# Second batch of an attention and mixture-of-experts kernel: the sign of a head's hash placed directly behind the hash

## The chip, the cores and the metric

The kernel runs on one core of a Trainium2 chip. The metric is the device time of one execution in microseconds (us); lower is better.

## The reference, cut to what matters

Two batches (B = 2) of 8 heads, 768 rows, 64 columns go through an attention in which a row sees only the keys of its own hash bucket. The bucket is the pattern of six signs of the row times a 64x6 matrix. The result, as 1536 rows of 512, goes through a dense mixture of four experts.

```python
q_bits = (np.einsum('bhsd,dk->bhsk', q, proj) > 0)
k_bits = (np.einsum('bhsd,dk->bhsk', k, proj) > 0)
mask = q_bucket[:, :, :, None] == k_bucket[:, :, None, :]
scores = np.where(mask, scale * q @ k^T, -1e9)
attn = softmax(scores);  x = attn @ v
for e in range(4):
    out += p[:, e:e+1] * (np.maximum(x @ w1[e], 0) @ w2[e])
```

## The kernel before, in words

**Heads and steps.** The 16 heads are numbered 0 to 15 here: head 8b + h is head h of batch b. `attention()` (L557) walks through all heads in steps of one 128-row tile of scores, six steps (t = 0 to 5) to a head. In each step it gives out the parts in the order `ORDER = "TXSUVMEYNRP"`: X turns an earlier tile of exponentials on VectorE (L458), S makes the scores of this step's tile (matmuls L368 and L370 on PE, minimum L375 on VectorE), E takes the exponential of the tile one step back (L391 on ScalarE), M multiplies by the reciprocal sums on GpSimd (L533), and P, last in the step, gives out one piece of the preparation of the **next** head. All engines execute their instructions in the order in which they were given out (`tc.manual_schedule()`), so the place in this order is the place in the engine's queue.

**Preparation of a head.** `prep_head` (L283) is a generator; one piece is taken in each step's P. For heads 2 to 8 and 11 to 15 (`BLOCKS`) the pieces are: t = 0 a transpose on VectorE (L293); t = 1 the split of q and k into a high and a low part (L230 on ScalarE, L231 on VectorE) and copies on GpSimd (L221); t = 2 the hash, six matmuls on PE (L315) into a PSUM tile `hps`, and a copy on GpSimd; t = 3 the sign of the hash (L324 on ScalarE: it reads `hps` and writes the bit rows of `k2`), then two GpSimd operations that make the bit rows of the other operand (L327, L335, the latter through the helper at L221). Heads 9 and 10 are turned on PE instead (L299), and have everything one step earlier: split at t = 0, hash at t = 1, sign and GpSimd operations at t = 2. The preparation issues no DMA; the loads are given out by P itself (L619, L621). The values that the generator yields (654, 978, 0) are only a budget for the mixing described next. `mixed(b, h)` (L357) is true for heads 0 to 8.

**What runs beside it.** While batch 0's attention runs, nothing of the experts but the split of the first weights does. After that the experts of batch 0 (`moe`, L740) and the attention of batch 1 are woven together (L998 to L1008): after each block of the experts (`yield 1960`: twelve matmuls L757 to L759 into a tile `mps`, Relu L763 on ScalarE, L764 on VectorE; or `yield 2600`: twelve matmuls L697 to L699, L691 on VectorE) as many pieces of the attention are taken as the budget allows. The weights are loaded (L647), split into a high part by VectorE (L665) and a low part by GpSimd (L658) meanwhile. The experts of batch 1 (`moe_fast`) come last and alone.

**PSUM.** Two pools: `ps2` with **two** buffers (`big`, L100), which score tiles `sps`, transposes `tps` and hashes `hps` share, and `ps1` with four (`one`, L103) for all else. A buffer is given back when the last instruction that reads it is done: L375 for a score tile, L324 for a hash. Which of two free buffers a new tile gets is settled when the program is built. The next head's scores need the sign's products only at t = 0 of that head.

Of the kernel before, what the change touches and what calls it, by code (L numbers as in the profile page):

```python
# [10 lines left out]
ACTF = mybir.ActivationFunctionType  # L11
# [7 lines left out]
SGN_SCALE = float(2**20)  # L19
# [30 lines left out]
def tile_lsh_attention__then__domain_moe(  # L50
# [11 lines left out]
    nc = tc.nc  # L62
    B, H, S, D = q.shape
# [12 lines left out]
    NH = S // 2  # L76
# [3 lines left out]
    MKE = MK + 2 * NB  # L80
    scale = 1.0 / float(D) ** 0.5
# [18 lines left out]
    def big(name):  # L100
        return ps2.tile([P, 2, 512], F32, tag="big", name=name)

    def one(name):  # L103
        return ps1.tile([P, 512], F32, tag="one", name=name)
# [3 lines left out]
    sgn_bias = const.tile([P, 1], F32, name="sgn_bias")  # L108
# [11 lines left out]
    def two(t):  # L120
        return t.rearrange("p (a n) -> p a n", a=2)
# [65 lines left out]
    def in_blocks(b, h):  # L187
        return b * H + h in BLOCKS
# [27 lines left out]
    def stack_tiles(b, h):  # L216
        heads[b, h] = tuple(stk.tile([P, S], F32R, tag=n, name=n) for n in ("q1", "al", "ah", "k2"))
        return heads[b, h]

    def copy_pool(dst, src):  # L220
        nc.gpsimd.tensor_scalar(out=dst, in0=src, scalar1=1.0, scalar2=1.0, op0=ALU.mult, op1=ALU.mult)  # L221
# [7 lines left out]
    def split_half(dst_hi, dst_lo, src):  # L229
        nc.scalar.activation(dst_hi, src, ACTF.Copy, scale=qk_scale)  # L230
        nc.vector.scalar_tensor_tensor(  # L231
            out=dst_lo, in0=src, scalar=qk_scale, in1=dst_hi.bitcast(F32), op0=ALU.mult, op1=ALU.subtract
        )
# [49 lines left out]
    def prep_head(b, h):  # L283
        second = (b, h) == (0, 1)
        if not second:
            tqk = loaded.pop((0, b, h))
        q1, al, ah, k2 = stack_tiles(b, h)
        if second:
            for ps, sl in zip(in_psum, halves):
                split_half(ah[:, sl], al[:, sl], ps[:, :NH])  # L290
        elif in_blocks(b, h):
            xt = ld.tile([P, S], F32, tag="tqk", name="xt")
            nc.vector.transpose(out=xt, in_=tqk.rearrange("p c r d -> p (c r d)"))  # L293
            yield 0
            split_half(two(ah), two(al), two(xt))
        else:
            ps = big("tps")
            for c in range(NT):
                nc.tensor.transpose(  # L299
                    ps[:, c // 3, (c % 3) * P : (c % 3 + 1) * P], tqk[:, c].rearrange("p a d -> p (a d)"), ident  # L300
                )
            split_half(two(ah), two(al), ps[:, :, :NH])
        for rows in (slice(0, D), slice(D, P)):
            copy_pool(q1[rows], ah[0:D].bitcast(F32))
        copy_pool(k2[0:D], ah[D:P].bitcast(F32))
        yield 654
        if second:
            yield 0
            ps = [one("hps1") for _ in range(2)]
        else:  # L310
            hps = big("hps")
            ps = [hps[:, i] for i in range(2)]
        for j, (w, a) in enumerate(((phi, ah), (plo, ah), (phi, al))):
            for i, sl in enumerate(halves):
                nc.tensor.matmul(ps[i][:MKE, :NH], w, a[:, sl], start=j == 0, stop=j == 2)  # L315
        copy_pool(ah[0:D], al[D:P].bitcast(F32))
        if second:
            for i, sl in enumerate(halves):
                nc.scalar.activation(
                    k2[D:MKE, sl], ps[i][D:MKE, :NH], ACTF.Sign, bias=sgn_bias[D:MKE], scale=SGN_SCALE  # L320
                )
        yield 978
        if not second:
            nc.scalar.activation(  # L324
                two(k2[D:MKE]), hps[D:MKE, :, :NH], ACTF.Sign, bias=sgn_bias[D:MKE], scale=SGN_SCALE
            )
        nc.gpsimd.tensor_scalar(  # L327
            out=al[D:MKE],
            in0=k2[D:MKE].bitcast(F32),
            scalar1=1.0,  # L330
            scalar2=bit_mul[D:MKE],
            op0=ALU.add,
            op1=ALU.mult,
        )
        copy_pool(k2[MQ:MQE], al[MK:MKE].bitcast(F32))  # L335
        yield 0
# [20 lines left out]
    def mixed(b, h):  # L357
        return b * H + h < LIGHT_FROM
# [198 lines left out]
    def attention():  # L557
# [3 lines left out]
        def do(op, i):  # L561
# [24 lines left out]
            elif op == "S":  # L586
                if i < n:
                    b, h, t = seq[i]
                    if t == 0:
                        x = hseq.index((b, h))  # L590
                        prep[0] = prep_head(*hseq[x + 1]) if x + 1 < len(hseq) else iter(())
                    stage_s(b, h, t)
                    return 652 + 4270 // NT
# [446 lines left out]
```

## Time and profile before

| | us |
|---|---|
| median of 3 runs | 745.59 (745.38 to 748.12) |
| the profiled execution, its own time | 746.74 |
| its span in the trace | 744.8 |
| PE busy | 721.7 (97%) |
| VectorE (DVE) busy | 472.6 (63%) |
| ScalarE (ACT) busy | 298.7 (40%) |
| GpSimd (POOL) busy | 306.9 (41%) |

How to read it: the span is the time between the first and the last instruction that the profiler recorded. Times of rows are us from its start. Engines work side by side, so busy times don't add up to the span. In a timeline a row has start, duration, engine, line, operation, output <- input, and in brackets how long the engine sat idle before it and what it waited for. PEclk is the granted TensorE clock as a share of full speed.

### The profile page before, as it was taken

How to read it: one execution, taken by the hardware profiler on the slowest of the kernel's cores; microseconds unless marked ns; L12 is line 12 of the kernel's file. 1: busy time of each engine (PE TensorE's matmuls, PEld its weight loads, DVE VectorE, ACT ScalarE, POOL GpSimd, SP SyncE). 2: the span in 40 equal slices, each digit the busy share in tenths (PEclk: the TensorE clock that was granted, in tenths of full speed). 3: DMA queues.
4: the chain of work that ended last, by engine and by line, in shares of the span. 5: the costliest groups of instructions: out<-in, count | busy, mean ns of one | idle time of the engine just before them, and what ended most of it. 6: DMA issues, size and time to landing. Idle time of an engine off the chain costs nothing.

```text
span 744.8 us, 10164 instructions
## 1 busy us (share of the span) xinstructions
PE 721.7 (97%) x3826; PEld 615.3 (83%) x3826; DVE 472.6 (63%) x781; ACT 298.7 (40%) x592; POOL 306.9 (41%) x279
## 2 busy tenths in 40 slices
PE   8988899999989999899999999999999999999998
PEld 6766566697987897879879888998989989899896
DVE  6677676546666666568563323798667686676763
ACT  6777677633232341332422010444334343343430
POOL 5349485423415441445142324754234342343420
PEclk9999999999999999999999999999999999999999
DMA  5224323504686797769767411243021130212302
GB/s 142 44 51 85 72 60 85 85 1 129 162 206 157 213 240 180 193 164 259 217 193 211 115 58 56 67 137 109 30 86 57 63 106 30 85 58 64 105 1 85
DMA packets 85504, 83.05 MB, mean 111 GB/s; under 512 B 49872, under 2 KB 52432, under 8 KB 85456
## 3 DMA queue, kind: packets, MB, share of 16 engines
q1 hardware_dynamic: 84432, 82.08, 40.8%
q8 instruction: 30, 0.49, 0.3%
q10 hardware_dynamic: 1024, 0.33, 0.2%
q14 instruction: 18, 0.15, 0.1%
HBM read 62.68 MB, written 19.71 MB: 111 GB/s over the span
## 4 chain that ended last, share of the span: by engine, by line
PE 87%; ACT 5%; DVE 4%; DMA 2%; issue 1%; POOL 0%; SPq 0%; DVEq 0%; POOLq 0%; ACTq 0%
PE mps L697 12%; PE mps L699 12%; PE mps L698 12%; PE pv L493 9%; PE mps L758 6%; PE mps L757 6%; PE mps L759 6%; PE sps L368 4%; PE sps L370 3%; PE ptps L438 2%; PE mps L912 2%; PE mps L908 2%; PE mps L911 2%; ACT p L391 2%; PE pd L908 2%; PE pa L912 2%
## 5 line engine op out<-in xcount | busy, mean ns | idle before, releaser
L697 PE MATMUL mps<-w2hi,hh 128*128 128x512 f32 (+1 forms) x388 | 150.7, 388 | 0.0
L699 PE MATMUL mps<-w2hi,hl 128*128 128x512 f32 (+1 forms) x388 | 150.5, 388 | 0.0
L698 PE MATMUL mps<-w2lo,hh 128*128 128x512 f32 (+1 forms) x388 | 150.4, 388 | 0.0
L375 DVE TENSOR_SCALAR_CACHE_REDUCE p<-sps 128x768 f32<-128x768 f32 x96 | 90.3, 941 | 32.9 <-PE sps L370 31.2
L391 ACT ACTIVATE p<-p,nb 128x768 f32<-128x768 f32 x96 | 89.5, 932 | 42.3 <-DVE p L375 41.8
L691 DVE SCALAR_TENSOR_TENSOR acc<-mps,pe,acc 128x512 f32<-128x512 f32 (+1 forms) x85 | 63.0, 741 | 63.0 <-PE mps L699 62.6
L763 ACT ACTIVATE hh<-mps 128x384 fp32r<-128x384 f32 x64 | 31.4, 490 | 178.5 <-PE mps L759 178.5
L758 PE MATMUL mps<-xs,w1hi 128*128 128x384 f32 x256 | 87.3, 341 | 0.6 <-POOL xs L538 0.6
L757 PE MATMUL mps<-xs,w1hi 128*128 128x384 f32 x256 | 87.7, 343 | 0.0
L759 PE MATMUL mps<-xs,w1lo 128*128 128x384 f32 x256 | 87.2, 341 | 0.0
L699 PEld LDWEIGHTS mps<-w2hi,hl 128*128 128x128 f32 x388 | 72.8, 188 | 15.6
L894 POOL TENSOR_TENSOR w2lo<-ws,w2hi 128x512 fp32r<-128x512 f32 x32 | 40.5, 1286 | 108.4 <-ACT w2hi L893 108.4
L698 PEld LDWEIGHTS mps<-w2lo,hh 128*128 128x128 f32 x388 | 72.9, 188 | 13.9
L697 PEld LDWEIGHTS mps<-w2hi,hh 128*128 128x128 f32 x388 | 72.8, 188 | 13.8
L764 DVE SCALAR_TENSOR_TENSOR hl<-mps,hh 128x384 fp32r<-128x384 f32 x64 | 35.5, 555 | 73.4 <-ACT hh L763 73.1
L658 POOL TENSOR_TENSOR w1lo<-ws,w1hi 128x512 fp32r<-128x512 f32 x32 | 42.5, 1328 | 79.6 <-DVE w1hi L665 36.1
L658 POOL TENSOR_TENSOR w2lo<-ws,w2hi 128x512 fp32r<-128x512 f32 x32 | 41.2, 1289 | 69.5 <-DVE w2hi L665 55.5
L493 PE MATMUL pv<-pt,tv 128*64 128x384 f32 x288 | 67.3, 492 | 0.0
L221 POOL TENSOR_SCALAR q<-ah 64x768 fp32r<-64x768 f32 (+1 forms) x33 | 32.4, 982 | 72.0 <-ACT ah L230 70.5
L368 PE MATMUL sps<-ah,q 128*128 128x384 f32 x192 | 54.5, 365 | 6.7 <-DVE p L375 3.7
L853 POOL TENSOR_TENSOR w1lo<-ws,w1hi 128x512 fp32r<-128x512 f32 x24 | 37.9, 1588 | 35.6 <-ACT w1hi L849 22.4
L493 PEld LDWEIGHTS pv<-pt,tv 128*64 128x64 f32 x288 | 24.8, 136 | 32.2 <-issue 31.8
(135 smaller groups left out, 1432.8 us busy)
## 6 DMA issues: line engine op xcount, KB each, us to landing
ws<-in_moe_w_dram SPq DMA_DIRECT2D x64, 512.0 KB, 4.0
scr<-t SPq DMA_DIRECT2D x14, 1152.0 KB, 8.7
pt<-scr SPq DMA_DIRECT2D x56, 288.0 KB, 6.1
tv<-in_v_dram SPq DMA_DIRECT2D x16, 192.0 KB, 4.5
out_dram<-acc SPq DMA_DIRECT2D x11, 256.0 KB, 2.0
rdb<-row SPq DMA_DIRECT2D x14, 192.0 KB, 5.2
tqk<-in_q_dram SPq DMA_DIRECT2D x26, 96.0 KB, 3.3
tqk<-in_k_dram SPq DMA_DIRECT2D x24, 96.0 KB, 3.4
```

What stands on the lines that cost most here:

```text
L368: nc.tensor.matmul(ps[:, i, :NH], q1[:, sl], k1[:, i * NH : (i + 1) * NH], start=True, stop=False)
L375: nc.vector.tensor_scalar(out=two(pt), in0=ps[:, :, :NH], scalar1=MASKED, scalar2=MASKED, op0=ALU.min, op1=ALU.min, accum_out=nb,)
L391: nc.scalar.activation(pt, pt, ACTF.Exp, bias=nb, scale=-1.0, accum_out=dens[b, h, r][:, o : o + 1])
L493: nc.tensor.matmul(dst, vvs[b, h][:, c], pts[b, h, g][c], start=c == 0, stop=c == NT - 1, tile_position=(0, g * D),)
L658: nc.gpsimd.tensor_tensor(out=lo[:, c - 1], in0=st[c - 1], in1=hi[:, c - 1].bitcast(F32), op=ALU.subtract)
L691: nc.vector.scalar_tensor_tensor(out=acc, in0=ps, scalar=pcol, in1=acc, op0=ALU.mult, op1=ALU.add)
L697: nc.tensor.matmul(ps, hh[:, ts], w2hi[:, f, cs], start=n == 0, stop=False)
L698: nc.tensor.matmul(ps, hh[:, ts], w2lo[:, f, cs], start=False, stop=False)
L699: nc.tensor.matmul(ps, hl[:, ts], w2hi[:, f, cs], start=False, stop=n == FC - 1)
L757: nc.tensor.matmul(ps[:, :SB], w1hi[:, kk, fs], xhi[b, kk][:, sl], start=kk == 0, stop=False)
L758: nc.tensor.matmul(ps[:, :SB], w1hi[:, kk, fs], xlo[b, kk][:, sl], start=False, stop=False)
L759: nc.tensor.matmul(ps[:, :SB], w1lo[:, kk, fs], xhi[b, kk][:, sl], start=False, stop=kk == KD - 1)
```

## The change

Heads 9 to 15: the sign stands directly behind the hash, in the same piece, so it is given out before the next step's parts instead of behind them. Heads 0 to 8 keep the order that they had. Heads 9 and 10 also get one empty piece more (`yield 0`) ahead of the two GpSimd operations, which so come one step later than before, at t = 3, as they do in heads 11 to 15, where they stay. Nothing is added to or removed from the computation.

```diff
         yield 654
+
+        def sign():
+            nc.scalar.activation(
+                two(k2[D:MKE]), hps[D:MKE, :, :NH], ACTF.Sign, bias=sgn_bias[D:MKE], scale=SGN_SCALE
+            )
+
         if second:
             yield 0
             ps = [one("hps1") for _ in range(2)]
...
+        if not mixed(b, h):
+            sign()
         yield 978
-        if not second:
-            nc.scalar.activation(
-                two(k2[D:MKE]), hps[D:MKE, :, :NH], ACTF.Sign, bias=sgn_bias[D:MKE], scale=SGN_SCALE
-            )
+        if b and h and not in_blocks(b, h):
+            yield 0
+        if mixed(b, h) and not second:
+            sign()
         nc.gpsimd.tensor_scalar(
             out=al[D:MKE],
...
```

## Rows read from the trace of the kernel before

**Rows 1.** The page: busy time, share of the span, instructions of each engine.

```profile
PE 721.7 (97%) x3826; PEld 615.3 (83%) x3826; DVE 472.6 (63%) x781; ACT 298.7 (40%) x592; POOL 306.9 (41%) x279
```

**Rows 2.** Waits of PE over the whole span: us in total, times, longest.

```profile
PE sps L368 <- DVE p L375: 3.7, 4, 2.3
PE sps L368 <- ACT k L324: 2.4, 1, 2.4
```

**Rows 3.** Stretches: length, then busy us of PE, PEld, DVE, ACT, POOL; PEclk; DMA.

```profile
180.00:210.00 30.00, 27.59 (x145) 23.99 (x144) 20.47 (x36) 9.06 (x19) 12.54 (x11) 1.00 0.72 176
240.00:270.00 30.00, 30.00 (x166) 26.42 (x165) 19.70 (x32) 10.33 (x22) 12.16 (x11) 1.00 0.83 228
300.00:330.00 30.00, 27.66 (x139) 23.84 (x139) 18.91 (x33) 9.03 (x19) 15.94 (x14) 0.94 0.65 176
```

**Rows 4.** Line L324, the sign: duration ns min/median/max, first and last start.

```profile
L324 ACT ACTIVATE k<-hps,sgn_bias x14: 895/896/900, 27.1 to 348.1; 44x768 fp32r<-44x768 f32 x14
```

**Rows 5.** Timeline of all engines while head 11 is prepared.

```profile
201.13 0.51 PE L315 MATMUL hps<-al,phi 128*108 128x384 f32 x2
...
201.39 0.93 ACT L391 ACTIVATE p<-p,nb 128x768 f32<-128x768 f32 x1
...
203.57 0.51 PE L368 MATMUL sps<-ah,q 128*128 128x384 f32 x2
203.77 0.49 ACT L763 ACTIVATE hh<-mps 128x384 fp32r<-128x384 f32 x1 [1.36 <-PE mps L759]
...
206.59 0.49 ACT L763 ACTIVATE hh<-mps 128x384 fp32r<-128x384 f32 x1 [2.32 <-PE mps L759]
206.97 0.93 ACT L391 ACTIVATE p<-p,nb 128x768 f32<-128x768 f32 x1
...
208.01 0.90 ACT L324 ACTIVATE k<-hps,sgn_bias 44x768 fp32r<-44x768 f32 x1
...
208.96 0.61 PE L368 MATMUL sps<-ah,q 128*128 128x384 f32 x2 [2.41 <-ACT k L324]
```

**Rows 6.** Stretches behind the two longest waits of PE, columns as in rows 3.

```profile
209.80:213.40 3.60, 3.60 (x14) 3.60 (x13) 0.97 (x2) 0.00 (x0) 1.01 (x2) 0.53 1.03 228
...
308.50:312.10 3.60, 3.60 (x14) 3.60 (x13) 2.17 (x4) 0.00 (x0) 2.45 (x2) 0.57 0.18 15
```

**Rows 7.** Timeline of all engines while head 14 is prepared.

```profile
302.60 0.93 ACT L391 ACTIVATE p<-p,nb 128x768 f32<-128x768 f32 x1
302.70 0.51 PE L315 MATMUL hps<-al,phi 128*108 128x384 f32 x2
...
305.43 0.43 DVE L665 CAST w2hi<-ws 128x512 fp32r<-128x512 f32 x1 [3.59 <-DMA ws<-in_moe_w_dram]
...
306.66 0.92 DVE L375 TENSOR_SCALAR_CACHE_REDUCE p<-sps 128x768 f32<-128x768 f32 x1
...
307.65 0.61 PE L368 MATMUL sps<-ah,q 128*128 128x384 f32 x2 [2.34 <-DVE p L375]
...
315.86 0.90 ACT L324 ACTIVATE k<-hps,sgn_bias 44x768 fp32r<-44x768 f32 x1
```

**Rows 8.** Timelines, heads 9 and 13: last hash matmuls and the next on ACT.

```profile
134.14 0.51 PE L315 MATMUL hps<-al,phi 128*108 128x384 f32 x2
...
135.02 0.49 ACT L444 ACTIVATE pth<-ptps 128x384 f32<-128x384 f32 x1 [1.16 <-PE ptps L438]
...
271.04 0.51 PE L315 MATMUL hps<-al,phi 128*108 128x384 f32 x2
...
271.22 0.94 ACT L391 ACTIVATE p<-p,nb 128x768 f32<-128x768 f32 x1 [2.03 <-DVE p L375]
```

**Rows 9.** Timelines of POOL and PE, preparation and first use of head 10.

```profile
171.15 0.92 POOL L327 TENSOR_SCALAR al<-k,bit_mul 44x768 fp32r<-44x768 f32 x1 [9.55 <-ACT k L324]
...
176.36 1.27 POOL L658 TENSOR_TENSOR w1lo<-ws,w1hi 128x512 fp32r<-128x512 f32 x1 [1.34 <-DVE w1hi L665]
...
186.85 0.52 PE L370 MATMUL sps<-k,al 76*128 76x384 f32 x2
```

## The prediction, made before the changed kernel ran

> **What bounds the kernel now.** I read the page first: PE is busy for 721.7 us, 97% of the span, and the next engine for 63% [rows 1]. So PE sets the end, and a change pays only what it takes out of PE's idle time or out of the time in which PE runs slowly. Next I read PE's waits. The sign is named there once, with 2.4 us before a score matmul; the minimum L375, which frees the buffers of score tiles, with 3.7 us in four waits, the longest 2.3 us [rows 2]. Third, the stretches: from 180 to 210 us and from 300 to 330 us PE is busy for 27.59 and 27.66 of 30 us, and a stretch between them is full [rows 3]. So in the part where the changed heads are prepared there are two gaps, and almost nothing else to win. The timelines show what each gap is.
>
> *Gap 1, head 11.* The last hash matmuls end at 201.64 (201.13 + 0.51). The sign could follow, but it stands behind the next step's parts: ACT does E at 201.39, a Relu at 203.77, one at 206.59, whose block of matmuls PE has only just finished, E again at 206.97, and the sign from 208.01 to 208.91. PE wants the hash's PSUM buffer for the next score tile and sits idle for 2.41 us until 208.96 [rows 5].
>
> *Gap 2, head 14.* The hash ends at 303.21, but the sign stands only at 315.86. All that time the hash holds one of the two `big` buffers, so score tiles share the other. The score at 307.65 waits 2.34 us for the minimum of the tile before it, at 306.66, which VectorE does late because it waited 3.59 us for weights to land at 305.43 [rows 7]. The trace names L375 as the releaser, yet the reason that there was no other buffer is the late sign.
>
> Behind both gaps PE runs slowly: the granted clock is 0.53 over the next 3.60 us and 0.57 over another 3.60 us, with 14 matmuls in each [rows 6], against 1.00 in the full stretch [rows 3]. That is 1.2 GHz for most of it where it had been 2.4. The loss is (1 - 0.53) x 3.60 = 1.69 us and (1 - 0.57) x 3.60 = 1.55 us.
>
> **The change part by part.** *Sign moved, heads 9 to 15.* Its length stays 0.90 us [rows 4]; no instruction is added. On ACT it now waits for the hash, and the next step's instructions queue behind it. It starts when the hash and the E before it are done.
> - Head 11: E ends at 202.32; the sign runs until about 203.3, before the Relu of 203.77 could start. PE would find the buffer free when it comes at 206.55 (208.96 - 2.41). Gap 1 goes: -2.41, and the slow clock behind it: -1.69. Sum -4.10.
> - Head 14: E ends at 303.53; the sign runs from about 303.6 to 304.5. PE comes to the score at 305.31 (307.65 - 2.34). If the score tile takes the hash's buffer, gap 2 goes: -2.34 and -1.55. Sum -3.89. The margin is 0.8 us. What is late next: the minimum at 306.66 still comes late, but the score after it would come about two blocks and a score later, so its buffer is then free.
> - Heads 9 and 13: here something on ACT is pushed back. In head 9 the hash ends at 134.65, the sign at 135.55, and the copy that started at 135.02 starts 0.53 us later; in head 13 the hash ends at 271.55, the sign at 272.45, and the E of 271.22 starts 1.23 us later [rows 8]. Bounds: nothing, if PE does not need their results at once, and 0.53 + 1.23 = 1.76 us, if all of it lands on PE. I take nothing: the old sign stood close behind these same instructions, so ACT's total up to there is unchanged, and PE did not wait for ACT there. If that cover goes, it costs the 1.76.
> - Heads 10, 12 and 15 are like head 11: the sign would end before ACT's next instruction starts, and PE shows no gap. Taken at 0.
>
> *GpSimd operations of heads 9 and 10, a step later.* In head 10 L327 stood at 171.15 after 9.55 us of waiting for the sign; PE first needs the product at 186.85. If two weight operations come ahead of it, it starts behind 177.63 (176.36 + 1.27), and with 0.92 us of its own and as much for the copy behind it it ends near 179.5, 7 us ahead of the need [rows 9]. Cost 0, at worst as far as the weight operations are now freed from waiting behind it, a small gain off the path. In heads 11 to 15 these two keep their place and get their input earlier. SP's queue is passed by nothing, since the preparation issues no DMA and the loads keep their steps. The extra piece yields 0, so the weaving with the experts stays as it is.
>
> *The clock.* The rows show a loss behind both gaps, so I take both. A sentence apart: the Trainium skill, page "TensorE: Matmul & The Clock Gate", Part 1, says that the clock drops to 1.2 GHz when PE has been idle and that the moment is not tied to the kernel, so that the slow stretch varies between runs; by it a run of before may have paid 2.41 + 2.34 = 4.75 us for the gaps alone, and the change would be worth that much to it instead of 7.99. Both gaps of this trace agree with the drop; that it varies no row here shows.
>
> **The sum.** -4.10 - 3.89 = -7.99 us. Against the profiled execution's own 746.74 us that is 738.75. The median of the three runs, 745.59, lies 1.15 us below it; the same sum from there would be 737.6. I keep 738.7.
>
> **The rivals.**
> 1. *Both gaps go* (my forecast): 738.7 us.
> 2. *Only gap 1 goes.* Which of two buffers a tile gets is settled when the program is built, so it need not be the one that is free first on the chip. In head 11 the score right behind the hash (203.57) did not take the hash's buffer; the one after that did [rows 5]. If head 14's score at 307.65 keeps the buffer of the tile before it, it keeps waiting for the minimum. Against it: with the sign done 3 us ahead of that minimum, the hash's buffer is by far the first one free. Time: 746.74 - 4.10 = 742.6.
> 3. *The wait changes hands.* With gap 2 gone PE is some 4 us nearer to the weights, which landed late there (3.59 us of waiting on VectorE), and waits for their low parts a stage later; or gap 1 reappears before a minimum. If one gap of the same size comes back with its slow clock, 3.89 to 4.10 us of the sum are lost and it is about 742.8; if both do, the time is that of before, 746.7. I take the latter as this rival's time, since the first is rival 2's.
> 4. *Slower: ACT blocked.* The sign now makes ACT wait for PE, and Relu, E and copies behind it wait too. It decides where PE needs ACT's next result before the sign's end. The price is one sign's length in each of the seven heads, 7 x 0.90 = 6.3 us, if the gaps stay: 753.0. Against it: only in two of seven heads does ACT have work in that time [rows 8]. The Trainium skill's page "PSUM — Partial Sum Buffer", section "Engine vs sequencer instructions", says that ScalarE's queue is strictly first in, first out, which is what makes this possible; no row here contradicts it.
> That the change does nothing is no rival of its own: ACT's order in the seven heads is different for certain.
>
> **How the numbers follow.** A measurement of this kernel can tell about 0.5% from no change, 3.7 us here; from the median that is 741.9 and 749.3. Chances: rival 1 60%, rival 2 22%, rival 3 11%, rival 4 7%. Rival 1 is faster by over 0.5%. Rival 2's 742.6, or 741.5 counted from the median, lies on the border: a third of it goes to faster. So faster 0.67, same 0.26, slower 0.07. The range begins at 736.9, the median less the sum and 0.7 us (half of the 1.4 us of L375's other three waits in rows 2, which a buffer that is free earlier may also save), and reaches to 743.2 to take in rival 2 with a third of the 1.76 us.
>
> **What would show it.** In the changed profile the sign's rows of heads 9 to 15 should start within 1 us of the end of their hash; PE's waits should no longer name L324, and the 2.3 us of L375 should be gone; the stretch 180 to 210 and the one that was 300 to 330 should be full at a clock of 1.00. If the wait for L375 of over 2 us is still there, rival 2 is right. If PE waits for L665, L658 or a landing instead, rival 3. If PE waits for L763, L391 or L444 in the seven heads, rival 4. A time above 744 us would make the forecast wrong, whatever the waits say.

## The result, and the profile after

The changed kernel takes 738.88 us in the median (738.63 to 739.72, four runs) against 746.04 us (745.38 to 748.12) of the kernel before (four runs; the 745.59 above is the median of three of them): a ratio of 0.9897, 95% interval 0.9874 to 0.9919. The profiled execution takes 738.97 us; that of before took 746.74. The forecast was 738.7, in a range of 736.9 to 743.2. Line numbers of the changed kernel are up to eight higher: the sign is now L309 (a helper that both places call), the hash L321, the scores L376 and L378, the minimum L383, the exponential E L399, Relu L771, the high part of the weights L673.

The page's busy line of the changed kernel, which answers to [rows 1]:

```profile
PE 719.0 (98%) x3826; PEld 614.4 (83%) x3826; DVE 472.5 (64%) x781; ACT 298.6 (41%) x592; POOL 306.7 (42%) x279
```

Busy time is that of before within 0.2 us on VectorE, ScalarE and GpSimd; weight loads (PEld) have 0.9 us less and PE has 2.7 us less (721.7 before). Matmuls that no longer run at the low clock would explain it: in the control run below, the same program with a clock of 1.00 throughout, PE has 718.3 us, 3.4 less than before, where the two slow stretches were worth 1.69 + 1.55 = 3.24. PE's waits from 120 to 445 us, as in [rows 2]:

```profile
PE hps L321 <- DVE al L231: 0.8, 1, 0.8
PE mps L766 <- POOL xs L546: 0.6, 1, 0.6
PE hps L321 <- ACT ah L230: 0.6, 1, 0.6
```

Neither the sign nor the minimum is in the list; both long waits are gone. The stretches of [rows 3], and one of batch 0:

```profile
180.00:210.00 30.00, 30.00 (x159) 26.69 (x158) 20.98 (x36) 9.79 (x20) 13.38 (x12) 1.00 0.72 174
...
300.00:330.00 30.00, 30.00 (x153) 25.29 (x153) 21.32 (x38) 9.92 (x20) 16.62 (x15) 1.00 0.73 176
20.00:40.00 20.00, 18.10 (x109) 13.41 (x107) 12.70 (x23) 13.86 (x31) 5.63 (x6) 0.91 0.20 40
```

The two stretches with the gaps are full, at a clock of 1.00. The third row holds a slow stretch in code that the change does not touch; more on it at the end.

Head 11 in the timeline (start, length, engine, line, operation; a wait stands in brackets), to be laid beside [rows 5]:

```profile
201.43 0.51 PE L321 MATMUL hps<-al,phi 128*108 128x384 f32 x2
...
201.69 0.93 ACT L399 ACTIVATE p<-p,nb 128x768 f32<-128x768 f32 x1
...
202.74 0.90 ACT L309 ACTIVATE k<-hps,sgn_bias 44x768 fp32r<-44x768 f32 x1
...
203.87 0.51 PE L376 MATMUL sps<-ah,q 128*128 128x384 f32 x2
...
206.69 0.51 PE L376 MATMUL sps<-ah,q 128*128 128x384 f32 x2
```

In head 11 the sign ends at 203.64, and the scores at 203.87 and 206.69 have no wait in brackets. Head 14 in the same view, to be laid beside [rows 7]:

```profile
298.78 0.51 PE L321 MATMUL hps<-al,phi 128*108 128x384 f32 x2
...
299.72 0.90 ACT L309 ACTIVATE k<-hps,sgn_bias 44x768 fp32r<-44x768 f32 x1
...
301.23 0.51 PE L376 MATMUL sps<-ah,q 128*128 128x384 f32 x2
301.52 0.43 DVE L673 CAST w2hi<-ws 128x512 fp32r<-128x512 f32 x1 [3.60 <-DMA ws<-in_moe_w_dram]
...
302.75 0.92 DVE L383 TENSOR_SCALAR_CACHE_REDUCE p<-sps 128x768 f32<-128x768 f32 x1
```

In head 14 VectorE is as late as before (3.60 us of waiting for the weights, the minimum at 302.75), but the score at 301.23 starts 1.5 us **ahead** of that minimum: it went into another buffer, in the program as built that of the hash, which the sign gave back at 300.62.

**A yardstick without batch 0's scatter.** The line of the first expert matmuls has the start of its first and of its last instruction. Between them lies the woven part, in which six of the seven heads are prepared (head 9 comes just ahead of it). Before and after:

```profile
L757 PE MATMUL mps<-xs,w1hi x256: 333/334/522, 145.6 to 476.1; 128*128 128x384 f32 x128
```

```profile
L765 PE MATMUL mps<-xs,w1hi x256: 333/334/443, 146.3 to 468.2; 128*128 128x384 f32 x128
```

The woven part took 476.1 - 145.6 = 330.5 us and takes 468.2 - 146.3 = 321.9 us: 8.6 us less. What lies ahead of it is 0.7 us longer in this pair of executions, what lies behind it the same (268.7 and 268.8 us). Whole times contain the attention of batch 0, and its end lies anywhere from 144.3 to 147.5 us in the profiles below that leave heads 2 to 8 alone; the woven part is the sharper measure. It is one execution each, but it repeats: 321.9 us again in the control run and 322.0 in the run without the empty piece.

### The profile page after: what moved, and what is told of

Same layout as the page of the kernel before. It is cut to its first block, busy times and chain, and to the rows that moved or that the text cites. A ratio compares the mean times of both kernels' runs of the same rounds, so it can differ in the third digit from the quotient of the medians.

```text
span 737.0 us, 10172 instructions
## 1 busy us (share of the span) xinstructions
PE 719.0 (98%) x3826; PEld 614.4 (83%) x3826; DVE 472.5 (64%) x781; ACT 298.6 (41%) x592; POOL 306.7 (42%) x279
## 4 chain that ended last, share of the span: by engine, by line
PE 90%; ACT 4%; DVE 4%; issue 1%; DMA 0%; POOL 0%; ACTq 0%; DVEq 0%; POOLq 0%
PE mps L705 12%; PE mps L707 12%; PE mps L706 12%; PE pv L501 9%; PE mps L766 6%; PE mps L765 6%; PE mps L767 6%; PE sps L376 4%; PE sps L378 3%; PE ptps L446 3%; PE mps L920 2%; PE mps L916 2%; PE mps L919 2%; ACT p L399 2%; PE pd L916 2%; PE pa L920 2%
## 5 line engine op out<-in xcount | busy, mean ns | idle before, releaser
L383 DVE TENSOR_SCALAR_CACHE_REDUCE p<-sps 128x768 f32<-128x768 f32 x96 | 90.3, 941 | 32.6 <-PE sps L378 30.9
L399 ACT ACTIVATE p<-p,nb 128x768 f32<-128x768 f32 x96 | 89.5, 932 | 34.4 <-DVE p L383 33.9
L771 ACT ACTIVATE hh<-mps 128x384 fp32r<-128x384 f32 x64 | 31.4, 490 | 162.3 <-PE mps L767 162.3
L766 PE MATMUL mps<-xs,w1hi 128*128 128x384 f32 x256 | 85.9, 336 | 0.6 <-POOL xs L546 0.6
L765 PE MATMUL mps<-xs,w1hi 128*128 128x384 f32 x256 | 86.4, 337 | 0.0
L221 POOL TENSOR_SCALAR q<-ah 64x768 fp32r<-64x768 f32 (+1 forms) x33 | 32.5, 984 | 73.2 <-ACT ah L230 71.8
L376 PE MATMUL sps<-ah,q 128*128 128x384 f32 x192 | 54.6, 366 | 1.4 <-DVE p L383 0.9
```

What stands on the lines that cost most here:

```text
L376: nc.tensor.matmul(ps[:, i, :NH], q1[:, sl], k1[:, i * NH : (i + 1) * NH], start=True, stop=False)
L383: nc.vector.tensor_scalar(out=two(pt), in0=ps[:, :, :NH], scalar1=MASKED, scalar2=MASKED, op0=ALU.min, op1=ALU.min, accum_out=nb,)
L399: nc.scalar.activation(pt, pt, ACTF.Exp, bias=nb, scale=-1.0, accum_out=dens[b, h, r][:, o : o + 1])
L765: nc.tensor.matmul(ps[:, :SB], w1hi[:, kk, fs], xhi[b, kk][:, sl], start=kk == 0, stop=False)
L766: nc.tensor.matmul(ps[:, :SB], w1hi[:, kk, fs], xlo[b, kk][:, sl], start=False, stop=False)
```

## The experiments

Every run was compared with the kernel before on its own chip; there its median was 746.67, 746.94 and 746.97 us in the three sets.

**Undo it for head 11 alone.**

```diff
+LATE = (11,)
...
-        if not mixed(b, h):
+        if not late(b, h):
             sign()
...
-        if mixed(b, h) and not second:
+        if late(b, h) and not second:
             sign()
...
+    def late(b, h):
+        return mixed(b, h) or b * H + h in LATE
```

> The changed kernel with the sign of head 11 alone put back a step. Theory (two gaps of PE, each made by a hash that holds one of the two big PSUM buffers until a late sign): gap 1 comes back, PE waits about 2.4 us for the sign before a score of head 10's last steps, and the time is 738.9 + 2.4 = 741.3 us, or 743.0 if the clock drops behind the gap as it did in the kernel before (1.7 us more). Rival (gap 1 was covered by something else that is late anyway, the whole gain came with head 14): 738.9. The stretch of head 14 stays full in both.

Measured: 743.09 us median (740.25 to 744.48), ratio 0.9949 (0.9930 to 0.9968). PE's longest wait from 120 us on:

```profile
PE sps L380 <- ACT k L310: 2.4, 1, 2.4
```

The line of the first expert matmuls:

```profile
L769 PE MATMUL mps<-xs,w1hi x256: 333/334/525, 144.3 to 470.6; 128*128 128x384 f32 x128
```

And the stretch behind the gap (third from the end: the granted clock):

```profile
208.00:211.60 3.60, 3.60 (x14) 3.60 (x13) 0.96 (x2) 0.00 (x0) 1.41 (x2) 0.53 1.05 227
```

Gap 1 is back with its slow clock. The woven part is 326.3 us, 4.4 more than in the changed kernel; the prediction had 4.10. The rival falls.

The slow clock does not come in every execution. By the mean granted clock of the whole run, the six are: 1.00, 740.25 us; 0.998, 741.42 and 742.28 us; 0.995, 743.90, 743.91 and 744.48 us. The profiled one is that with 741.42; its one slow stretch is the one shown, behind the gap. The three at 0.995 are some 4 us dearer than the one at 1.00, and this stretch alone does not make that: it is worth (1 - 0.53) x 3.60 = 1.69 us, while 0.005 of 740 us is 3.7 us by estimate. Where the rest lay in them is open; in the profile of the next run, also at 0.995, a second slow stretch lies in batch 0, from 20 to 40 us.

**Undo it for head 14 alone.** The same edit with `LATE = (14,)`.

> The changed kernel with the sign of head 14 alone put back a step. Theory: gap 2 comes back, and the trace names the minimum of the tile before, not the sign, as what PE waits for (about 2.3 us); 738.9 + 2.3 = 741.2 us, or 742.8 if the clock drops. Rival (the wait for the minimum has nothing to do with the sign): 738.9, without a wait of over 1 us.

Measured: 741.80 us (740.04 to 743.28), ratio 0.9936 (0.9921 to 0.9951). PE's longest wait from 120 us on:

```profile
PE sps L380 <- DVE p L387: 2.2, 1, 2.2
```

The line of the first expert matmuls:

```profile
L769 PE MATMUL mps<-xs,w1hi x256: 333/334/522, 146.8 to 472.5; 128*128 128x384 f32 x128
```

As expected the trace does not name the sign: it names the minimum, although only the sign was moved. The slow clock is back as well, 0.53 where [rows 6] had 0.57:

```profile
304.90:308.50 3.60, 3.60 (x13) 3.60 (x13) 2.21 (x5) 0.00 (x0) 2.45 (x2) 0.53 0.27 20
```

The woven part is 325.7 us, 3.8 more than in the changed kernel (predicted 3.89).

**The buffer alone.** Every instruction stays where the changed kernel has it; from the score behind head 14's hash on, each tile of the two-buffer pool goes to the other buffer, given by a list of zeros and ones (`SIDES`, one digit for each tile). Against the changed kernel nothing but buffers and three of PE's waits differ.

```diff
+    n_big = [0]
...
-        return ps2.tile([P, 2, 512], F32, tag="big", name=name)
+        side = SIDES[n_big[0]]
+        n_big[0] += 1
+        return ps2.tile([P, 2, 512], F32, tag="big" + side, name=name, bufs=1)
```

> The changed kernel, every instruction in the same place and every sign early, but from the score behind head 14's hash on, each big tile gets the other PSUM buffer: that score takes the buffer of the tile before it instead of the hash's. Theory (it is the buffer that PE waited for): a wait of about 2.3 us for the minimum comes back before that score and the time is 741.2 us, or 742.8 with the clock's drop. Rival (what matters is when ACT does the sign and what it does earlier for it, not the buffer): 738.9 us and no such wait.

Measured: 742.02 us (740.49 to 743.49), ratio 0.9937 (0.9921 to 0.9954). The timeline around head 14's hash:

```profile
300.07 0.90 ACT L317 ACTIVATE k<-hps,sgn_bias 44x768 fp32r<-44x768 f32 x1
...
302.96 0.92 DVE L391 TENSOR_SCALAR_CACHE_REDUCE p<-sps 128x768 f32<-128x768 f32 x1
...
303.95 0.61 PE L384 MATMUL sps<-ah,q 128*128 128x384 f32 x2 [2.21 <-DVE p L391]
```

The line of the first expert matmuls:

```profile
L773 PE MATMUL mps<-xs,w1hi x256: 333/334/522, 146.7 to 472.3; 128*128 128x384 f32 x128
```

The sign is done at 300.97, early as in the changed kernel, and PE still waits 2.21 us, because its score stands in line for the buffer of the tile before. The woven part is 325.6 us, 3.7 more. So what the early sign gives at head 14 is a free buffer, and nothing else of it counts.

**Only heads 11 and 14 early**, all else as before the change: `LATE = (9, 10, 12, 13, 15)`, and no empty piece.

> The kernel before with the sign moved in heads 11 and 14 alone; heads 9, 10, 12, 13 and 15 and the GpSimd operations of heads 9 and 10 as before. Theory: these two heads are all of the gain, 738.9 us (738 to 740). Rival (the other five heads or the two GpSimd operations matter too): 740 to 744 us, with waits of PE in their steps.

Measured: 739.41 us (738.38 to 740.76), ratio 0.9907 (0.9892 to 0.9922). These two heads are nearly all of the gain: the woven part is 470.0 - 147.5 = 322.5 us, 8.0 less than before (the two terms of the forecast come to 7.99) and 0.6 more than with all seven. What remains on PE is one wait of 0.4 us for the minimum (`PE sps L378 <- DVE p L385: 0.4, 1, 0.4` in the waits from 120 us on), which the changed kernel does not have.

**Without the empty piece.**

```diff
-        if b and h and not in_blocks(b, h):
-            yield 0
```

> The changed kernel without the empty piece, so that the two GpSimd operations of heads 9 and 10 stay a step earlier, where they were before. Theory: 738.9 us (within 0.5), because these products are needed some 14 us later and nothing on PE waits for GpSimd there. Rival (the step's delay is what lets the weights' low parts pass): PE waits for L666 or L546 in batch 0's first expert blocks, 739.5 to 742.

Measured: 738.65 us (737.04 to 739.29), ratio 0.9894 (0.9876 to 0.9912). **The changed kernel again**, in the same set:

> The changed kernel itself, beside the three others on the same chip: 738.9 us, no wait of PE for the sign or for L375 of over 1 us from 120 us on, the granted clock 1.00 there.

Measured: 738.68 us (738.08 to 738.81), ratio 0.9895 (0.9878 to 0.9911). The two medians differ by 0.03 us and the woven parts by 0.1 (322.0 and 321.9): the later GpSimd operations of heads 9 and 10 show no effect either way.

These runs also show the clock's part without a timeline. The 32 executions of the kernel before in the three sets have a mean granted clock of 0.993 to 0.998 each; of the eight of the changed kernel, result and control together, five have 1.00, one 0.999 and two 0.997. The means are 0.9959 and 0.9991; by estimate the difference of 0.0032 is worth 2.4 us in 740, of the 7 to 8 that were gained.

**Is it idling that brings the slow clock?** The run with head 11 late, and sixteen transposes of the identity, read by nobody, right before the score that waits.

```diff
+        if (b, h, t) == (1, 2, 4):
+            fill = one("fill")
+            for _ in range(16):
+                nc.tensor.transpose(fill[:, :P], ident, ident)
```

> The run late11 (sign of head 11 late, PE idle for 2.4 us) with sixteen extra 128x128 transposes of the identity, whose result nobody reads, right before the score that waits: PE does some 2.2 us of work where it sat idle. Theory (the slow clock behind a gap comes from PE having been idle in it): the granted clock is 1.00 in every profile behind the gap and the time 738.7 + 2.4 = 741.1 us, with little spread, against 740.3 to 744.5 us in late11. Rival (the slow stretch has another cause, or waiting itself costs more than the gap): as late11, 743, with a stretch at about 0.53.

Measured: 740.31 us (739.64 to 742.11), ratio 0.9915 (0.9897 to 0.9934). PE in the timeline:

```profile
205.44 1.91 PE L380 MATMUL fill<-ident 128*128 128x128 f32 x16
208.02 0.62 PE L384 MATMUL sps<-ah,q 128*128 128x384 f32 x2 [0.67 <-ACT k L310]
```

The stretch behind the gap:

```profile
208.00:211.60 3.60, 3.58 (x20) 3.58 (x21) 1.02 (x3) 0.46 (x1) 1.74 (x2) 1.00 1.02 251
```

The line of the first expert matmuls:

```profile
L773 PE MATMUL mps<-xs,w1hi x256: 333/334/443, 145.1 to 469.4; 128*128 128x384 f32 x128
```

The score waits about as long as in late11, but PE works for 1.91 us of it, and behind it 20 matmuls fall into 3.60 us at a clock of 1.00, where 14 did at 0.53. The woven part is 324.3 us: 2.4 above the changed kernel, the gap's bare length, and 2.0 below late11. Useless work in the gap won back the slow clock, not the gap. The other executions agree: five of six have a clock of 0.999 or 1.00, against one of six in late11. The sixth had 0.997 and 742.11 us; it has no trace, so where its slow stretch lay is open.

**The early sign in batch 0 too** (heads 2 to 8).

```diff
-        if not mixed(b, h):
+        if not second:
             sign()
...
-        if mixed(b, h) and not second:
-            sign()
```

> The changed kernel with the sign directly behind the hash in heads 2 to 8 as well. There the hash itself waits for the split (PE waits of 0.6 to 1.1 us before L321), and ACT has copies and exponentials queued behind. Theory of the slower rival (ACT is blocked where it has work queued and PE needs it soon): each of seven heads loses 0.5 to 1.5 us, 742 to 749 us, and PE waits for copies or exponentials of ACT. Rival (the wait of ACT is hidden behind PE's twelve pv matmuls of about 4 us): 738.9 us or a little less, since the score behind the hash finds a buffer (0.9 us of waits for L383 there).

Measured: 740.35 us (739.15 to 741.46), ratio 0.9918 (0.9902 to 0.9934): 1.7 us worse than the changed kernel in its set. PE's waits over the whole span:

```profile
PE hps L321 <- DVE al L231: 5.4, 7, 0.8
PE hps L321 <- ACT ah L230: 4.6, 7, 1.1
PE sps L374 <- ACT k L309: 2.4, 6, 0.6
```

The third row is new: in batch 0 the score behind the hash waits for the sign, now the last thing that gives its buffer back. The slower rival has the right sign, but not the size: 0.24 us a head (1.7 / 7) where 0.5 to 1.5 were expected. Part of the 1.7 us may be the clock, as the three executions at 1.00 took 739.15 to 739.75 us and the three at 0.997 and 0.998 took 740.94 to 741.46; but from the hash of head 3 to that of head 8 the trace has 80.70 us against 79.10 in the changed kernel and 79.84 in the control, 0.2 to 0.3 us a head with the clock at 1.00. And what PE waits for is the sign itself and not, as expected, the copies and exponentials behind it.

**The hash of batch 0 a step later.**

```diff
+        if mixed(b, h) and not second:
+            yield 0
         if second:
```

> The changed kernel with the hash of heads 2 to 8 given a step later (an empty piece ahead of it), its sign and products a step later too. The remaining idle time of PE lies in batch 0, where 9.2 us of waits stand before the hash (L321) for the split on ACT and VectorE. Theory (these waits are paid by PE, and the split is done a step later): 738.9 - 9.2 = 730 us at best, 730 to 735. Rival (VectorE and ACT, busy two thirds of the time there, set the pace of batch 0, so the wait moves to copies, exponentials or the minimum): 737 to 740 us.

Measured: 742.44 us (741.67 to 742.89), ratio 0.9945 (0.9932 to 0.9959), 3.8 us worse than the changed kernel. The theory falls, and the rival's size with it:

```profile
PE sps L380 <- POOL k L221: 3.4, 2, 2.5
PE sps L378 <- DVE p L385: 3.4, 9, 0.4
PE pv L503 <- DVE pth L452: 3.4, 6, 0.6
PE ptps L448 <- ACT pth L454: 3.2, 6, 0.6
```

Of the 9.2 us of waits before the hash all but 0.8 are gone, and 13.4 us (0.9 in the changed kernel) stand elsewhere: for GpSimd's products, which now come too late for the next head, and for minima and copies. **Both at once**, hash a step later and every sign right behind it:

> The run hash_later with every sign right behind its hash, so that in batch 0 hash and sign stand a step after the split and the GpSimd products come at the same step as the hash. Theory: the 3.4 us of PE's waits for GpSimd's products in hash_later go, 742.4 - 3.4 = 739.0 us, no better than the changed kernel, because the waits for copies and minima (some 11 us there) stay. Rival (with the products early enough the 9.2 us of waits before the hash are a gain after all): 730 to 736 us.

Measured: 740.57 us (740.16 to 741.11), ratio 0.9913 (0.9895 to 0.9931). No better than the changed kernel, as expected, but not for the reason given: the waits for GpSimd's products did not go, they are the largest in its profile (`PE sps L378 <- POOL k L221: 5.1, 3, 3.1`). Why the earlier sign does not bring them forward stays open. No version here is clearly faster than the changed kernel.

## Why the prediction was right, point by point

*Gap 1, -4.10 us.* Held. The sign ends at 203.64 (forecast 203.3, from a hash that ended 0.3 us earlier), the wait is gone, and putting head 11 back costs 4.4 us of the woven part. One detail was off: I expected the score right behind the hash to keep the other buffer and the next one, some 5 us behind the hash, to find the hash's free. In the program as built the score right behind takes the hash's buffer, so the sign was done only 0.2 us before it was needed (203.64 and 203.87), not some 3 us. Neither score waits, but that is closer than the forecast knew.

*Gap 2, -3.89 us.* Held, with its reason. The open question was which buffer the score would take. In the trace it starts ahead of the minimum that it waited for before, and the run with the buffers exchanged shows that this alone decides: 3.7 us come back with the sign early. That run is rival 2 made real, and at 742.02 us it lies 0.6 us from the 742.6 worked out for it.

*The clock, 1.69 and 1.55 us of the sum.* Held for the executions profiled: behind the gaps of late11 and late14 the clock is 0.53, with work in the gap of late11 it is 1.00, and the woven parts of late11 without and with that work differ by 2.0 us. The page "TensorE: Matmul & The Clock Gate" of the Trainium skill, Part 1, says that the clock falls after idling, and that the moment of a change does not depend on the program alone. The runs agree with both: the clock fell behind gaps and stayed with work in one, and the six executions of late11 have mean clocks from 1.00 to 0.995. So the gain of one run over another is not fixed. A run of before that paid for the gaps alone, which the forecast held possible, is not among the 32.

*Heads 9 and 13 at 0, heads 10, 12 and 15 at 0.* Nearly: the three-head and two-head parts together are 0.6 us (the run with heads 11 and 14 alone), 0.4 of it a small wait for the minimum, the kind for which the range's lower end kept 0.7 us. No new wait for ACT appears on PE (the 0.6 us for L230 in the list above, at 119.90, is one that before has too, at 118.63 and so ahead of 120 us). Head 9 lies ahead of the woven part, where executions scatter too much to show 0.5 us.

*GpSimd operations, the extra piece: 0.* Held: 738.65 without, 738.68 with it.

*Rival 4, 0.90 us a head.* It could not decide here, since five of the seven heads leave ACT idle at that time. Where ACT is busy, in batch 0, it is real but smaller: 0.2 to 0.3 us a head.

*The total.* -7.99 forecast, -7.77 between the profiled executions (746.74 - 738.97): -8.6 in the woven part and +0.7 ahead of it. Between the medians it is -7.16 (746.04 and 738.88, four runs each) and -8.26 in the control's set (746.94 and 738.68). The agreement to 0.2 us is partly luck: the woven part gave 0.6 us more than forecast, and the part ahead of it, of which the change touches only head 9, happened to take 0.7 back.

## What to carry to other kernels

Where two buffers of PSUM rotate, the reader that gives one back is as urgent as the next writer: look in its engine's queue for what stands ahead of it, and put it directly behind its producer if that engine is idle there. A wait is named after the instruction that ended it; ask which other buffer could have been free and who held it, as the sign did while the trace named the minimum. The same move costs time where the reader's engine has work queued and PE itself arrives late, and taking a wait away by moving its instruction later can raise others by more than it was.

## What the runs showed that I had not expected

A gap of 2.4 us costs 4.4 us of the woven part with the slow clock behind it, and 2.4 when 1.91 us of it are filled with transposes that nobody reads. Not every gap brings the slow clock: in hash_later PE waited 2.47 us for a product of GpSimd, until 68.95, and the clock of the next stretch was 1.00; in early_and_later it waited 3.06 us for one, until 67.37, and the clock was 0.50:

```profile
69.60:73.20 3.60, 3.24 (x25) 2.93 (x24) 3.26 (x6) 3.25 (x8) 1.21 (x2) 1.00 0.12 27
```

```profile
68.40:72.00 3.60, 3.60 (x17) 3.50 (x16) 2.80 (x5) 2.79 (x6) 0.27 (x1) 0.50 0.10 18
```

A slow stretch also appeared in the changed kernel's profile at 20 to 40 us (clock 0.91), where the profile of before has none and nothing was changed. PE had just waited 1.13 and 0.77 us there; in the control it waited 1.11 and 0.77 us at the same place, without a slow stretch. The profiles of late14, force14, early11_14 and all_early have it too, at 0.91; those of the other runs do not. It costs time where it lies: from the hash of head 2 to that of head 3 the changed kernel's profile takes 17.09 us (23.71 to 40.80); the control's, at a clock of 1.00, takes 15.86 (23.98 to 39.84) and that of before 15.19 (23.64 to 38.83). By the start of the woven part only 0.2 us of it is left against the control (146.3 and 146.1), because the rest of batch 0 was 0.8 us shorter and the start before it 0.3. So the scatter of batch 0, and with it that of whole times, is in part the clock's.
